# A gated linear recurrence with a dense layer behind it: the first unit's last pair of heads handled in two halves, and other rank shifts in the plan

## The chip, the cores and the metric

The kernel runs on one core of one Trainium2 chip. Such a core has five engines with a queue of instructions each: TensorE (PE, matrix products), VectorE (DVE), ScalarE (ACT), GpSimd (POOL) and SyncE (SP, which only issues transfers here). ACT and POOL issue transfers too. The metric is the device time of one execution in microseconds (us); the median of three runs is compared. The profile is of one further execution, so its own time stands beside them.

## The reference

Two layers follow each other, all in float32:

```python
# q, k, v, a_re, a_im: (4, 8, 768, 48); the state S is a complex 48x48 matrix per batch and head
mag = sqrt(a_re**2 + a_im**2);  scale = minimum(mag, 0.999) / (mag + 1e-06)
for t in range(768):
    S = (a[t] * scale[t])[:, None] * S + outer(k[t], v[t])      # a complex, k and v real
    y[t] = q[t] @ real(S)
x = y as rows of tokens                                          # (3072, 384)
out = maximum(x @ w_in, 0)**2 @ w_out                            # 384 -> 2048 -> 384
```

## The kernel before

The tokens are cut into 6 units of 512 (`L`). A unit goes through these stages:

- `load(n)`: a, q, k and v are fetched. For the first unit the weights are fetched as well, in 16 pieces of 768 KB (`fetch`, issued by POOL, line 817); they lie in memory as 64-bit floats, and `convert` turns each into float32 with one or two steps on ACT (lines 830 and 834) and two or three on DVE (lines 836, 840, 843).
- `chain(n)`: the decays are normalised (lines 936 to 982; ACT and DVE take turns, and each step waits for the one before it), multiplied together within groups of four steps (lines 992 to 1000), scanned over the whole unit (`scan`, lines 1138 to 1205, with transposes on PE, line 1046, and copies of them on ACT, lines 1061 and 1227), and applied to q and k (lines 1266 to 1280). Everything is done for two halves of the heads, z = 0 and 1.
- `pairs(n)`: the 8 heads are handled as 4 pairs. Per pair: operands are turned to the right layout (for the first two units by PE, line 1382, with copies on ACT, line 1386), score products (PE, line 1400) are masked by DVE into `A` (line 1403), `keep` makes the states `St` that are carried between the four steps of 128 tokens (PE line 1428, DVE lines 1437 and 1439; its operand `KC` is gathered by small transfers, line 1321), and `mix` forms the pair's output in one PSUM bank, `yp`: 14 products, step by step over j = 0 to 3 (lines 1452 and 1456). ACT copies `yp` to a buffer `yt` in token order (line 1462, one copy of 112 x 512), and SP sends the rows of each head to their place in `xT` (line 1470). `xT` holds the unit's activations, features on partitions, in three chunks of 128 features; the last pair of a unit ends the third chunk.
- `dense(n, grp)`: for two groups of 256 tokens, the products with w_in (PE, line 1492), relu and square on ACT (lines 1523 and 1524), and the products with w_out. In the first group of each unit some of these products run on their first two chunks before the third chunk of `xT` is there (`split`, in the first two units more of them, on spare banks). From unit 1 on, the products with w_out take halves (line 1600); in eight of the groups (`seven`) one of eight block products is saved by sums and differences that DVE forms (line 1615, results added at line 1624).

None of this stands in the order of the program. Every piece of work is a `step` of a `Plan` with an engine, an assumed duration, keys that it reads and writes, and a rank. `Plan.order` plays the steps through as a list scheduler: on the engine that can start first it takes the ready step of the lowest rank, and the instructions are then issued in that order, so that each engine's queue has a fixed order. Where PE would stop for longer than 0.8 us of the assumed time, idle matmuls on a spare bank are put in (line 735). `plan.shift` (line 1740) adds numbers to the ranks of groups of steps or of single steps, and so moves them in the queues. The real waits are set by the data, not by the plan's assumed times.

The lines of the last stage of a pair:

```python
y = take("yt", 2)
step("ACT", ac(L) + 0.5, [("yp",)], [("yt", y)], lambda: act.copy(...))      # line 1462
...
dma(sp, [("yt", y)], [("xT", n % 2, r // C)], lambda ...: sp.dma_start(...)) # line 1470
```

Of the kernel before, what the change touches and what calls it, by code (L numbers as in the profile page):

```python
# [480 lines left out]
class Plan:  # L481
# [49 lines left out]
    def order(self):  # L531
        steps = self.steps
        users = [[] for _ in steps]
        left = []
        for n, s in enumerate(steps):
            left.append(len(s[2]))
            for d in s[2]:
                users[d].append(n)
        engines = {s[0] for s in steps}
        free = {e: 0.0 for e in engines}  # L540
        wait = {e: [] for e in engines}
        done, start, at = {}, {}, {}
        bus, warm = 0.0, 6.0
        self.fill = {}

        def ready(n):
            e = steps[n][0]
            t = 0.0
            for d in steps[n][2]:
                same = steps[d][0] == e and steps[d][5] is None  # L550
                hop = 0.0 if same else self.HOP[steps[d][0]]
                if e == "PE" and not same and done[d] > 100.0:
                    paired = steps[d][5] is not None and steps[n][6]
                    hop += self.SLACK if paired else self.MARGIN
                t = max(t, done[d] + hop)
            at[n] = t
            wait[e].append(n)

        for n in range(len(steps)):
            if not left[n]:  # L560
                ready(n)
        for _ in steps:
            best = None
            for e in engines:
                if not wait[e]:
                    continue
                t = max(free[e], min(at[n] for n in wait[e]))
                if best is None or t < best[0]:
                    best = (t, e)
            t, e = best  # L570
            n = min((n for n in wait[e] if at[n] <= t), key=lambda n: (steps[n][4], n))
            wait[e].remove(n)
            _, dur, _, _, _, wire, _ = steps[n]
            start[n] = t
            if e == "PE":

                stop = t - free[e]
                spare = [b for b in self.lives if self.spare(b, done, free[e])]
                if spare and stop > self.FILL:
                    self.fill[n] = int((stop - 0.3) / self.EACH), spare[0]  # L580
                elif stop > self.STOP:
                    warm = t + self.COLD
                if t < warm:
                    dur += min(dur, 0.5 * (warm - t))
            free[e] = t + dur
            if wire is None:
                done[n] = t + dur
            else:
                lat, size = wire
                bus = max(bus, t + dur) + size / self.RATE  # L590
                done[n] = max(bus, t + dur) + lat
            for m in users[n]:
                left[m] -= 1
                if not left[m]:
                    ready(m)
        self.start, self.done = start, done
        return sorted(start, key=lambda n: (start[n], n))
# [24 lines left out]
def fast_path(ctx, tc, q, k, v, a_re, a_im, moe_w_in, moe_w_out, out, flag):  # L622
# [5 lines left out]
    B, H, S, D = q.shape  # L628
    C = 128
    W = 4  # L630
    L = W * C
    NU = B * S // L
    NP = H // 2
# [3 lines left out]
    NM = DM // C  # L637
# [12 lines left out]
    dve, pool, act, sp = nc.vector, nc.gpsimd, nc.scalar, nc.sync  # L650
    pe = nc.tensor
# [5 lines left out]
    def sb(name, n, dtype=F32, rows=C):  # L657
        return const.tile([rows, n], dtype, name=name)

    w1 = sb("w1", NM * FF).rearrange("p (i m f) -> p i m f", m=NM, f=2 * C)  # L660
# [9 lines left out]
    QT = [sb(f"QT{s}", 16 * C) for s in range(2)] + [TT[:, 0:16 * C]]  # L670
# [10 lines left out]
    St = [sb(f"St{s}", 3 * 2 * D) for s in range(2)]  # L681
    yts = [sb(f"yt{s}", L) for s in range(2)]
# [3 lines left out]
    xT = sb("xT", 2 * NM * L).rearrange("p (n m t) -> p n m t", n=2, m=NM)  # L686
# [11 lines left out]
                                                           r=2, b=2)  # L698
# [8 lines left out]
            for n in ("d0", "d1", "d2", "sc0", "sc1", "tr0", "tr1", "yp")}  # L707
    ypair = bank["yp"]
# [7 lines left out]
                     in_=turn_.rearrange("p (k x w) -> p k x w", w=4, x=4))  # L716
# [22 lines left out]
    def vs(n):  # L739
        return n % 2 if n < ROOM else 0  # L740
# [7 lines left out]
    def ac(n):  # L748
        return n / 1200.0 + 0.18
# [3 lines left out]
    def step(*args, **kw):  # L753
        return plan.add(*args, **kw)
# [4 lines left out]
    def dma(q, reads, writes, fn, rank, size, lat=1.8, group=None):  # L759
        name, dur = ("POOL", 0.55) if q is pool else ("SP" if q is sp else "ACT", 0.6)  # L760
        step(name, dur, reads, writes, fn, rank, (lat, size), group)
# [575 lines left out]
    def pairs(n, which):  # L1337
# [106 lines left out]
        def mix(i):  # L1444
            T = QT[got["T", i]].rearrange("p (i k h t) -> p i k h t", i=W, k=2, h=2)[0:R]
            at, s = got["S", i]
            aa = [As[got["A", i, h]].rearrange("p (j t) -> p j t", j=W) for h in range(2)]

            def go():
                for j in range(W):  # L1450
                    for h in range(2):
                        pe.matmul(ypair[64 * h:64 * h + D, ts(j, C)], lhsT=v5[:, j, 2 * i + h],  # L1452
                                  rhs=aa[h][:, j], start=True, stop=at[j] is None)
                    for h in range(2):
                        if at[j] is not None:
                            pe.matmul(ypair[64 * h:64 * h + D, ts(j, C)], lhsT=at[j][:, h],  # L1456
                                      rhs=T[:, j, 0, h], start=False, stop=True)
            step("PE", 2.0, [("A", got["A", i, h]) for h in range(2)]
                 + [("v", vs(n)), ("QT", got["T", i]), ("St", s), ("S", n % 2, i)],
                 [("yp",)], go, rank)  # L1460
            y = take("yt", 2)
            step("ACT", ac(L) + 0.5, [("yp",)], [("yt", y)], lambda: act.copy(  # L1462
                out=yts[y][0:64 + D].rearrange("p (j t c) -> p j c t", j=W, c=W),
                in_=ypair[0:64 + D].rearrange("p (j c t) -> p j c t", j=W, c=W)), rank)
            for h in range(2):
                r, end = (2 * i + h) * D, (2 * i + h + 1) * D
                p = 64 * h
                while r < end:
                    m = min(end - r, C - r % C)
                    dma(sp, [("yt", y)], [("xT", n % 2, r // C)], lambda r=r, m=m, p=p: sp.dma_start(  # L1470
                        out=xT[r % C:r % C + m, n % 2, r // C],
                        in_=yts[y][p:p + m]), rank, m * 2048, 2.4, group=n)
                    r, p = r + m, p + m

        for i in which:
            (turn_pe if n < EARLY else turn)(i)
# [7 lines left out]
    def dense(n, grp):  # L1484
# [14 lines left out]
        for f2 in range(NF // 2):  # L1499
# [4 lines left out]
            tiles.append((s, o.rearrange("p (f t) -> p f t", f=2)))  # L1504
            blocks.append((f2, b, ps, o, s))
        split = 3 + len(spare) if grp == 0 else 0
        for f2, b, ps, o, s in blocks[:split]:
            f = fs[f2][0]
            step("PE", 0.87, [("w1", f // FP)] + [("xT", n % 2, m) for m in range(NM - 1)],
                 [(b,)], part_of(f, ps[:, 0], range(NM - 1)), rank)  # L1510
        for f2, b, ps, o, s in blocks:
            for j in range(2):
                f = fs[f2][j]
                late = f2 < split and j == 0
                step("PE", 0.43 if late else 1.3,
                     [("w1", f // FP)] + [("xT", n % 2, m) for m in range(NM)]
                     + ([(b,)] if late or j else [])
                     + ([(b, "y")] if f2 < split and j else []),
                     [(b, "y")] if late else [(b,)] if j == 0 else [(b, "x")],
                     part_of(f, ps[:, j], (NM - 1,) if late else range(NM)), rank)  # L1520

            def relu(o=o, ps=bank[b]):
                act.activation(out=o, in_=ps, func=AF.Relu)  # L1523
                act.activation(out=o, in_=o, func=AF.Square)  # L1524
            step("ACT", 2 * ac(2 * G), [(b, "x"), (b,), (b, "y")],
                 [(b,)] + [("g", s, r) for r in range(4)], relu, (0, n))
# [209 lines left out]
    for i in range(2 * NPIECE):  # L1736
# [1 line left out]
    verdict()  # L1738

    plan.shift(  # L1740
        groups={51: 101.97, 77: 100.01, 80: 2.93, 100: -0.9, 159: -2.64, 161: 0.18, 183: 98.76,
            190: -200.92, 192: 0.69, 217: 103.2, 232: 0.28, 234: 103.28, 258: 1.25, 297: 0.64,
            352: 0.34, 354: 0.6, 372: 0.17, 394: -2.31, 396: -101.12, 411: -201.73},
        single={48: 0.43, 244: 2.93, 358: 0.46, 425: 4.98, 481: -297.85, 584: 0.23, 603: -197.29,
            731: 103.3, 809: 200.47, 856: 8.98, 911: 0.46, 1263: -97.94, 1415: -0.29,
            1677: -97.83, 1749: 1.33, 1753: 98.01, 2212: -0.63})
    with tc.manual_schedule():
        bad = plan.emit(flag[0:1, 0:1])
    return bad
# [53 lines left out]
```

## Time and profile before

| what | us |
|---|---|
| median of 3 runs | 702.49 |
| lowest and highest run | 701.89 and 705.13 |
| the profiled execution | 705.98 |
| its span, first to last instruction | 704.2 |
| PE busy | 685.2 (97%) |
| DVE busy | 572.1 (81%) |
| ACT busy | 347.9 (49%) |
| first dense product / last product | 98.99 / 697.9 |
| idle matmuls of line 735, all before 97.3 | 61.1 |

A row of a timeline gives the start and the length of a run of like instructions, the engine, the line, the operation, what it writes and reads, the count, and in brackets how long the engine sat idle before it and what ended that. Rows of PE overlap a little, since the end of a product in the pipeline is modelled. The list of waits sums such idle times by the line that waited and the work that released it: total, number of times, longest.

### The profile page before, as it was taken

The page shows a single profiled execution, that of the slowest core. Times are in us where ns is not written, and L with a number is a line of the kernel's source. Part 1 is how long each engine was busy: PE and PEld are TensorE (multiplying, and loading weights), DVE is VectorE, ACT ScalarE, POOL GpSimd, SP SyncE. Part 2 cuts the span into 40 slices and gives each one's busy share as a digit, 9 for nine tenths or more (in the row PEclk, how much of TensorE's full clock was granted, in tenths as well). Part 3 has the DMA queues.
Part 4 walks back from the last instruction along what each step waited for, and adds up shares of the span by engine and source line. Part 5 has one row for each costly group of instructions (what it writes and reads, how often), then busy time and mean ns, then how long its engine had stood idle before and what let it go on. Part 6 is the DMA issues. An engine that isn't in the chain of part 4 may idle for free.

```text
span 704.2 us, 12518 instructions
## 1 busy us (share of the span) xinstructions
PE 685.2 (97%) x4562; PEld 622.7 (88%) x4562; DVE 572.1 (81%) x1173; ACT 347.9 (49%) x578; POOL 175.7 (25%) x334
## 2 busy tenths in 40 slices
PE   9998889999999999999999999999999999999996
PEld 9998878767788999998998998998989989999996
DVE  5989899999888789997898598998599998337721
ACT  6693468955485534376424557324657242132230
POOL 6502553052400003305044050033130033032200
PEclk9999899999999999999999999999999999999999
DMA  9741459220630004735037570036550035288600
GB/s 276 220 178 26 105 133 292 76 68 20 171 104 23 1 13 123 197 78 155 0 96 197 127 154 12 1 91 179 136 158 1 19 86 136 65 282 282 208 2 27
DMA packets 56647, 79.58 MB, mean 113 GB/s; under 512 B 10976, under 2 KB 38752, under 8 KB 56576
## 3 DMA queue, kind: packets, MB, share of 16 engines
q0 software_dynamic: 15232, 40.72, 19.1%
q1 hardware_dynamic: 37072, 32.89, 18.4%
q10 hardware_dynamic: 4272, 5.08, 2.7%
q8 instruction: 38, 0.62, 0.4%
q14 instruction: 33, 0.27, 0.1%
HBM read 48.76 MB, written 4.72 MB: 76 GB/s over the span
## 4 chain that ended last, share of the span: by engine, by line
PE 63%; DVE 24%; DMA 4%; issue 3%; ACT 3%; SPq 1%; POOL 1%; ACTq 0%; DVEq 0%
PE d L1492 24%; PE d L1600 20%; PE sc L1400 4%; DVE f L1266 3%; PE d L1538 3%; DVE f L1280 3%; PE yp L1452 3%; PE tr L1428 2%; PE yp L1456 2%; DVE aq L1270 2%; PE tr L1492 1%; DMA aq<-in_a_im_dram 1%; DMA KC<-f 1%; PE sc L1492 1%; DVE f L992 1%
## 5 line engine op out<-in xcount | busy, mean ns | idle before, releaser
L1492 PE MATMUL d<-xT,w 128*128 128x256 f32 x1056 | 236.3, 381 | 3.1 <-issue 2.1
L1492 PEld LDWEIGHTS d<-xT,w 128*128 128x128 f32 x1056 | 199.0, 190 | 31.7 <-issue 3.5
L1600 PE MATMUL d<-w,g 128*128 128x192 f32 x768 | 132.7, 328 | 0.0
L1600 PEld LDWEIGHTS d<-w,g 128*128 128x128 f32 x768 | 124.9, 190 | 1.5 <-issue 0.9
L1523 ACT ACTIVATE g<-d 128x512 f32<-128x512 f32 x88 | 52.1, 592 | 120.6 <-PE d L1492 88.9
L1321 POOL DMA_DIRECT2D KC<-f x160 | 78.4, 498 | 112.0 <-issue 56.0
L1561 POOL DMA_DIRECT2D out_dram<-ot x22 | 12.6, 572 | 241.4 <-DVE ot L1624 145.1
L1600 PE MATMUL d<-T,g 128*128 128x192 f32 x384 | 66.8, 327 | 0.7 <-DVE g L1615 0.7
L1600 PEld LDWEIGHTS d<-T,g 128*128 128x128 f32 x384 | 62.8, 190 | 1.3 <-DVE g L1615 1.0
L735 PE MATMUL d<-ident 128*128 128x128 f32 x520 | 61.1, 281 | 1.5 <-POOL ident masks.py:199 1.5
L910 POOL DMA_DIRECT2D v<-in_v_dram x80 | 46.4, 587 | 64.7 <-PE yp L1452 21.0
L1524 ACT ACTIVATE g<-g 128x512 f32<-128x512 f32 x96 | 60.5, 631 | 3.0
L735 PEld LDWEIGHTS d<-ident 128*128 128x128 f32 x520 | 60.5, 198 | 1.5 <-POOL ident masks.py:199 1.5
L1615 DVE TENSOR_TENSOR g<-g 128x512 f32<-128x512 f32 x64 | 43.1, 684 | 22.3 <-ACT g L1524 15.3
L1400 PE MATMUL sc<-QT 96*128 96x128 f32 x368 | 47.9, 285 | 1.2 <-ACT QT L1386 1.2
L1462 ACT COPY yt<-yp 112x512 f32<-112x512 f32 x24 | 26.1, 1089 | 43.5 <-PE yp L1456 43.5
L1400 PEld LDWEIGHTS sc<-QT 96*128 96x128 f32 x368 | 45.0, 198 | 3.0 <-ACT QT L1386 1.6
L1266 DVE TENSOR_TENSOR f<-aq,xn 128x384 f32<-128x384 f32 (+1 forms) x64 | 45.0, 748 | 2.0 <-ACT xn L1227 1.9
L1280 DVE TENSOR_TENSOR f<-aq 128x384 f32<-128x384 f32 (+1 forms) x64 | 44.9, 752 | 0.6
L1538 PE MATMUL d<-w,g 128*128 128x384 f32 x128 | 44.3, 488 | 0.0
L1403 DVE TENSOR_TENSOR A<-sc,mask 128x512 f32<-128x512 f32 x45 | 29.7, 680 | 15.1 <-PE sc L1400 15.0
L992 DVE TENSOR_TENSOR f<-aq 128x384 f32<-128x384 f32 x72 | 36.9, 553 | 0.9
(195 smaller groups left out, 993.5 us busy)
## 6 DMA issues: line engine op xcount, KB each, us to landing
QT<-aq SPq DMA_DIRECT2D x128, 64.0 KB, 2.1
f<-in_moe_w_in_dram POOLq DMA_DIRECT2D x8, 768.0 KB, 7.1
f<-in_moe_w_out_dram POOLq DMA_DIRECT2D x8, 768.0 KB, 6.4
KC<-f POOLq DMA_DIRECT2D x104, 48.0 KB, 2.7
out_dram<-ot POOLq DMA_DIRECT2D x22, 192.0 KB, 2.4
QT<-aq ACTq DMA_DIRECT2D x64, 64.0 KB, 2.5
v<-in_v_dram POOLq DMA_DIRECT2D x80, 48.0 KB, 2.9
xT<-yt SPq DMA_DIRECT2D x36, 96.0 KB, 2.4
```

The lines of the kernel that those rows point to most:

```text
L735: plan = Plan(lambda b: pe.matmul(bank[b][:, 0:C], lhsT=ident, rhs=ident, start=True, stop=True), ["d2", "d1", "d0"], lambda ap: tc.nc.val ...
L910: lambda i=i, c=c, src=src: pool.dma_start(out=t[32 * c:32 * c + 32, i], in_=src[c]), vrank, 32 * 1536, 4.0,
L992: dve.tensor_tensor(out=f, in0=a[:, :, :, c - 1], in1=a[:, j, :, c].unsqueeze(1).to_broadcast([C, 2, HH, D]), op=ALU.mult)
L1266: lambda j=j, r=r: dve.tensor_tensor(out=f4[:, j, r], in0=a[:, r], in1=over(j), op=ALU.mult), late[z])
L1280: lambda j=j, r=r, o=o: dve.tensor_tensor(out=o[:, :, :, r * D:(r + 1) * D], in0=qk[:, j], in1=a[:, r], op=ALU.mult), late[z])
L1321: lambda i=i, c=c, queue=queue: queue.dma_start(out=kc[32 * c:32 * c + 32, i], in_=nat[32 * i:32 * i + 32, c]),
L1400: pe.matmul(sa[:, j], lhsT=T[:, j, 1, h], rhs=T[:, j, 0, h], start=True, stop=True)
L1492: pe.matmul(ps, lhsT=w1[:, f // FP, m, ts(f % FP, C)], rhs=xT[:, n % 2, m, ts(grp, G)], start=(m == 0), stop=(m == NM - 1))
L1523: act.activation(out=o, in_=ps, func=AF.Relu)
L1524: act.activation(out=o, in_=o, func=AF.Square)
L1538: pe.matmul(ps, lhsT=gt[:, f % 2, ts(i, C)], rhs=w2[:, f], start=(f == 0), stop=(f == NF - 1))
L1600: pe.matmul(bank[b][:, 0:DH], lhsT=g4[:, r, j], rhs=w(j), start=first and j == 0, stop=last and j == NT - 1)
```

## The change

- `mix`: for the first unit's last pair (`n == 0 and i == NP - 1`), the work is cut in two halves of the steps, j = 0, 1 and j = 2, 3. Each half has its own PE step, its own copy out of `yp` (112 x 256) and its own two transfers to `xT`, of 256 columns each. The rows of the second head of that pair go out on ACT's queue, not on SP's. All other pairs stay as they were.
- For the plan, `xT` gets one more key, "lower", for the third chunk's first half in the first unit; the first group of the dense layer of that unit depends on it and no longer on the whole chunk.
- The engines are gone through in a fixed order in `Plan.order`, where before it was a set.
- The numbers of `plan.shift` are others, and more: 38 groups and 28 single steps, before 20 and 17.

```diff
-        engines = {s[0] for s in steps}
+        engines = ("PE", "DVE", "POOL", "SP", "ACT")
...
+            cut = 2 if n == 0 and i == NP - 1 else 1
             y = take("yt", 2)
+            for u in range(cut):
+                js = range(u * W // cut, (u + 1) * W // cut)
+
+                def go(js=js):
+                    for j in js:
...
+                banks = [("yp", b) for b in range(2) if cut == 1 or b == u]
+                step("PE", 2.0 / cut, [("A", got["A", i, h]) for h in range(2)]
+                     + [("v", vs(n)), ("QT", got["T", i]), ("St", s), ("S", n % 2, i)],
+                     banks, go, rank)
+                sl = slice(js[0], js[-1] + 1)
+                mine = [("yt", y)] + ([("yt", y, 1)] if u else [])
+                step("ACT", ac(L // cut) + 0.5 / cut, banks + mine[:u], mine[u:], lambda sl=sl: act.copy(
+                         out=yts[y][0:64 + D].rearrange("p (j t c) -> p j c t", j=W, c=W)[:, sl],
+                         in_=ypair[0:64 + D].rearrange("p (j c t) -> p j c t", j=W, c=W)[:, sl]),
+                     rank)
+                xs = slice(js[0] * C, (js[-1] + 1) * C)
...
+                        queue = act if cut > 1 and h else sp
+                        writes = [("xT", n % 2, r // C)] if cut == 1 or u else []
+                        if n % 2 == 0 and r // C == NM - 1 and (cut == 1 or u == 0):
+                            writes.append(("xT", 0, NM - 1, "lower"))
+                        dma(queue, mine, writes,
+                            lambda r=r, m=m, p=p, xs=xs, queue=queue: queue.dma_start(
+                                out=xT[r % C:r % C + m, n % 2, r // C, xs],
+                                in_=yts[y][p:p + m, xs]), rank, m * 2048 // cut, 2.4, group=n)
...
+        def xk(m):
+            return ("xT", n % 2, m, "lower") if (n, grp, m) == (0, 0, NM - 1) else ("xT", n % 2, m)
...
-            step("PE", 0.87, [("w1", f // FP)] + [("xT", n % 2, m) for m in range(NM - 1)],
+            step("PE", 0.87, [("w1", f // FP)] + [xk(m) for m in range(NM - 1)],
...
-                     [("w1", f // FP)] + [("xT", n % 2, m) for m in range(NM)]
+                     [("w1", f // FP)] + [xk(m) for m in range(NM)]
...
     plan.shift(
-        groups={51: 101.97, 77: 100.01, 80: 2.93, 100: -0.9, 159: -2.64, 161: 0.18, 183: 98.76,
...
+        groups={9: -102.88, 43: 0.17, 51: 104.25, 54: -106, 77: 100.01, 101: -0.9, 105: 5.24,
...
```

The later lines move down with it: line 1462 becomes 1471, 1470 becomes 1486, 1492 becomes 1508, 1600 becomes 1619, 1615 becomes 1634.

## The prediction

> **What bounds the kernel now.** I read the busy shares by stage first, then the waits of TensorE, then the timelines round the first unit's last pair. The stages:
>
> ```profile
> 0.00:56.00 56.00, 54.16 (x465) 54.00 (x466) 45.28 (x105) 41.83 (x63) 22.05 (x49) 1.00 0.67 212
> 56.00:98.00 42.00, 38.15 (x360) 35.56 (x360) 38.75 (x81) 16.63 (x27) 15.68 (x32) 0.92 0.35 83
> 98.00:106.00 8.00, 5.43 (x36) 4.17 (x33) 7.86 (x11) 5.53 (x8) 7.64 (x14) 1.00 0.67 152
> 106.00:240.00 134.00, 132.07 (x727) 104.72 (x727) 118.71 (x248) 94.12 (x158) 29.38 (x53) 1.00 0.36 99
> 240.00:430.00 190.00, 188.82 (x1290) 175.93 (x1289) 166.22 (x337) 92.90 (x158) 50.59 (x96) 1.00 0.43 107
> 430.00:600.00 170.00, 168.68 (x1110) 156.72 (x1109) 149.32 (x312) 74.51 (x130) 36.20 (x70) 1.00 0.32 85
> 600.00:698.00 98.00, 97.89 (x588) 91.56 (x586) 45.65 (x87) 22.44 (x36) 14.16 (x21) 1.00 0.47 153
> ```
>
> The columns are the stretch, its length, then busy us of PE, PEld, DVE, ACT and POOL, the granted clock, the DMA share and GB/s. To 56 us PE's time is idle matmuls (line 735) and DVE works off the first unit's chain. From 106 to 698 PE is busy for 132.07 + 188.82 + 168.68 + 97.89 = 587.5 of 592 us: 4.5 us of waiting in all. DVE beside it has about 12% free until 600, so in that stretch either engine can make the other wait. A gain can come from two places only: an earlier start of the dense work near 105 us, and those 4.5 us. The start:
>
> ```profile
> 98.91 0.84 ACT L963 ACTIVATE f<-f 128x768 f32<-128x768 f32 x1 [4.37 <-DVE f L958]
> 99.66 0.83 ACT L970 ACTIVATE f<-f 128x768 f32<-128x768 f32 x1
> 100.39 1.12 ACT L1462 COPY yt<-yp 112x512 f32<-112x512 f32 x1
> ...
> 101.54 1.17 SPq L1470 DMA_DIRECT2D xT<-yt  x2
> ...
> 102.43 1.03 PE L1492 MATMUL sc<-xT,w 128*128 128x256 f32 x4
> 105.52 2.40 PE L1492 MATMUL d<-xT,w 128*128 128x256 f32 x10 [2.07 <-issue]
> ```
>
> The last mix ends at 99.07, but ACT has two steps of the next unit ahead of the copy, one of which waits for DVE (line 958). The copy ends at 101.5, the second DMA goes out at 102.1 and lands some 3.3 us later, and PE, which has done what needs only the first two chunks of xT, waits 2.07 us.
>
> **The change, part by part.** Places of after come from the order of its built instructions, durations from the trace of before.
>
> DVE up to the last pair. Before, DVE waits here:
>
> ```profile
> 36.43 0.35 DVE L1020 TENSOR_TENSOR f<-f 128x192 f32<-128x192 f32 x1 [1.17 <-issue]
> ...
> 87.47 0.25 DVE L1437 COPY St<-tr 96x96 f32<-96x96 f32 x1 [0.78 <-PE tr L1428]
> ```
>
> After puts a weight step (line 840, 0.95) into the first, and line 947 (0.94) of the next unit ahead of the second. The scan in between is longer: lines 1020 and 1026 (2.9 us together) now stand inside it, and a line 836 (0.55) ahead of the second inner chain. That 0.55 is covered, as PE's first block of idle matmuls ends only at 35.4, later than the chain at 32.9. The second block has 71 idle matmuls, not 59: 12 x 2 x 0.113 = 2.7 us more, ending at about 52.1 where the transposed operand is there at about 51.6; this 0.5 us on PE is covered by three weight steps on DVE (2.3 us). So line 1266 starts at 56.3 instead of 55.74, with one weight step more done. From there both run the same apply steps, so the last line 1280 of the unit ends at 86.65 + 0.5 = 87.15. Then after has 947 (0.88), three St steps (0.9), 843 (0.9), two mask multiplies (line 1403, 1.3): 91.1. Then one St step (0.25), 836 (0.47), 956, 958, 840 and 843 (0.9 each), and the last two mask multiplies (1.25): 96.65, against 97.27 before. By then after has line 958 (0.95) done as well, which before came after it. Total: DVE is about 1.5 us ahead.
>
> ACT. After, line 963 can start when 958 ends, 91.1 + 0.25 + 0.47 + 1.8 = 93.6, then itself (0.84), the third pair's copy (1.05), 970, 972 and 980 (0.83, 0.85, 1.07): ACT is free at 98.2. Mix begins with the masks, and a line 836 (0.5) now stands ahead of the St copies that its second step needs, so it lasts 2.2 us, not 1.9, and ends at 98.8.
>
> The halves. [...] The row: before, the 112x512 copy follows the last matmul of yp. [...] yp is one bank. As built, the first half's copy indeed waits for the last matmul of the mix and the second half's for nothing. By columns alone the first copy could start when ACT is free, at 98.2; by bank at 98.85. I take 98.85: the halved mix buys nothing. The halved copy costs about 0.55 us (between 0.52, half of 1.04, and 0.65 if a fixed part stays), so the first half is in SBUF at 99.4 instead of 101.5.
>
> The DMAs. Two become four, of half the bytes; one of each pair is on ACT's queue. [...]
>
> ```profile
> xT<-yt SPq DMA_DIRECT2D x36, 96.0 KB, 2.4
> xT<-yt SPq DMA_DIRECT2D x12, 64.0 KB, 2.1
> xT<-yt SPq DMA_DIRECT2D x12, 32.0 KB, 2.6
> ```
>
> 32 KB takes no less than 96 KB, so half a row saves no latency. I take 2.4 from issue to landing, bounds 1.9 and 4.0 (the extremes of this window). The lower half is there at 99.45 + 2.4 to 3.3 = 101.9 to 102.8, against 105.4. Price of the ACT queue: two issues of 0.6 us stand ahead of line 944 (1.5 us) of the next unit, which then ends near 102.8; DVE needs it at about 104.2, so 1.4 us of cover; without it line 947 and the last weight pieces would be late by 1.2.
>
> PE. Partial blocks start when pair 2's rows have landed, about 99.0. Three take 2.6 us, to 101.6. The fourth needs weight piece 4, which DVE finishes at 96.65 + 0.5 + 0.8 + 0.95 + 1.75 + 0.5 + 0.9 + 0.9 = 102.9, because after puts lines 974 and 977 ahead of it. So PE waits 1.3 us there, a new wait in the place of the old, and goes on to full blocks at 102.9 + 0.86 = 103.8 instead of 105.52. Start: **1.7 us earlier** (bounds 0 and 2.7: DMA at 4.0 with its issue at 101, and no wait for the weights). Later pieces come at 106.0, 107.4 and 108.8, each ahead of its block. The lower key of xT changes no wait: groups of 256 columns read what they read.
>
> Fetches on POOL: one later piece comes ahead of line 910's loads, so these end near 36 instead of 33.5; first use is at 75. DMA issues elsewhere stay as many.
>
> The new ranks after 106. PE's work is the same to the instruction, so only its 4.5 us of waiting can change:
>
> ```profile
> PE tr L1046 <- DVE xn L1205: 1.3, 2, 0.9
> PE yp L1452 <- DVE A L1403: 0.9, 3, 0.5
> PE d L1600 <- DVE g L1615: 0.7, 1, 0.7
> PE tr L1382 <- DVE St L1437: 0.7, 1, 0.7
> ```
>
> With PE 1.7 and DVE 1.5 earlier I compare how far each consumer and its producer moved in their queues. Second unit's line 1205 stands 0.9 earlier, its consumer unmoved: the wait of 0.93 falls to about 0.2. In the third unit PE's consumers of lines 1205 and 1403 stand 1.3 earlier, the producers 0 and 0.3 later: about 1.4 more of waiting. In the units after it the sums of line 1615 stand 1.6 to 5 us of DVE work later, while the products on them stay where they were to 1.3 us; part is taken up by DVE's own waits there (0.5 to 1.7 each). I put 0.5 net on that, bounds -1 and +5. Sum: -1.7 - 0.7 + 1.4 + 0.5 = -0.5, and since a wait once taken delays PE against DVE and shortens the next, the +1.4 and +0.5 count about two thirds: **-1.1 us**. The tail after 698 keeps its order. The profiled execution, 705.98 us with a span of 704.2, would become 704.9 with 703.1; the median 702.49 becomes 701.4.
>
> **Rivals.** (1) The ranks also clear the later waits: the start's 1.7 us plus 2 to 4 of the 4.5 us give 696.8 to 698.8, say 698. For it: unit 2's scan and several products move the right way. Against: DVE is as full as before. (2) Slower: the sums of line 1615. In three sevens between 400 and 520 us they were done only 0.2 to 1.8 us ahead of the product that reads them; they move back by 1.6 to 5 us of DVE work. At 2 us unhidden in each, 6 - 1.7 = 4.3 us are lost: 706.8. It decides from about 1.7 us per product group. (3) The change does nothing: DMA landing in 4.0 us or the weight piece later than 104.5 leaves the start at 105.5, with the later waits about as they were: 702.5.
>
> **How the numbers follow.** The start's gain in part (701.4): 0.38. Rival 1 (698): 0.36. Rival 2 (706.8): 0.20. Rival 3 (702.5): 0.06. The first, with a spread of its own of 2.3 us (698.9 to 703.7, from the bounds of the start and two thirds of those of the sums that lie on its side), and rival 3 are within 0.5% of 702.49, that is 3.5 us, about what a measurement of this kernel tells from no change; rival 1 is below, rival 2 above. So faster 0.36, same 0.44, slower 0.20. The predicted time is that of the likeliest, 701.4. The range for 8 in 10 reaches from the best price of rival 1 to that of rival 2, 696.8 to 706.8; what is left out is the upper half of rival 2 and what neither list has.
>
> **What would show it.** Right: the first half's copy (line 1471) starts near 98.9, right behind the last mix; PE's full blocks (line 1508) begin near 103.8, with a wait for DVE rather than for xT just ahead; PE's waits between there and the end sum to 4 to 6 us. Wrong: a copy that starts before the mix ends; landing times over 3.5 us for the half rows; waits of line 1619 for line 1634 above 3 us in sum (rival 2), or PE's waits below 2.5 (rival 1).

## The result, and the profile after

The changed kernel takes 706.45 us (median of 11 runs, 704.48 to 712.47) against 704.04 (11 runs, 701.89 to 705.67; 702.49 was the median of the first three): ratio **1.0068**, 95% interval 1.005 to 1.0086. It became slower by about 4.8 us, where a gain of 1.1 us, to 701.4, was forecast. The medians are only 2.4 us apart, because that of the changed kernel falls into the quicker of two groups of runs; the means, 708.45 and 703.83, are 4.6 us apart. The 706.45 lies inside the range of 696.8 to 706.8, but the sign is wrong, and the mechanism of the one rival that ends there is wrong too, as will be seen.

The runs of the changed kernel fall into two groups, and the mean granted clock of TensorE tells them apart: six runs at 704.5 to 706.5 us with a clock of 0.994 to 0.997, and five at 711.0 to 712.5 with 0.983 to 0.986. Their means are 705.74 and 711.71: the first group is 1.9 us above the kernel before, the second another 6.0. The profiled execution (711.0, span 709.3) is of the second group. That is not a disturbance from outside: the experiments remove and bring back these clock drops by the order of the kernel's own instructions (no clock under 0.992 where the first one puts that order back, down to 0.987 where the second brings it into the kernel before).

Two answers of the trace of the changed kernel, by stretches (columns as in the prediction: stretch, length, busy us of PE, PEld, DVE, ACT and POOL, granted clock, DMA share, GB/s). The stages of the forecast:

```profile
106.00:240.00 134.00, 132.56 (x735) 105.60 (x734) 119.30 (x253) 94.34 (x159) 30.78 (x55) 1.00 0.35 98
240.00:430.00 190.00, 189.36 (x1292) 176.07 (x1291) 166.05 (x340) 96.25 (x166) 50.59 (x96) 1.00 0.43 107
430.00:600.00 170.00, 167.34 (x1064) 155.02 (x1062) 144.80 (x297) 69.55 (x119) 36.09 (x70) 0.96 0.32 84
```

and the end of the last row in steps of 10 us:

```profile
570.00:580.00 10.00, 10.00 (x51) 8.97 (x50) 9.93 (x12) 3.70 (x7) 8.82 (x19) 1.00 0.68 176
580.00:590.00 10.00, 8.22 (x75) 7.65 (x75) 3.94 (x11) 1.15 (x2) 2.93 (x7) 0.81 0.40 108
590.00:600.00 10.00, 10.00 (x74) 9.36 (x70) 2.65 (x7) 1.07 (x1) 0.00 (x0) 0.51 0.40 98
```

To 580 us nothing is lost. Then PE stands still for 10 - 8.22 = 1.8 us, and the clock goes to half for (0.19 x 10 + 0.49 x 10) / 0.5 = 13.6 us (in the trace's record of the clock from 586.15 to 599.80), which costs up to 6.8 us of work. In the kernel before the same place looks so:

```profile
580.00:600.00 20.00, 20.00 (x192) 19.05 (x192) 16.93 (x32) 4.96 (x7) 5.85 (x12) 1.00 0.56 137
```

How far the work has come can be counted by the 96 squares of the dense layer on ACT (line 1543, before 1524). The 7th is 1.1 us earlier in the changed kernel (121.10 against 122.20), the 77th 2.5 us earlier (573.37 against 575.87), the 83rd 5.2 us later (633.40 against 628.16). So the whole loss of the profiled execution, 7.7 us, arises between the 77th and the 83rd square, where the last unit's pairs are worked on. TensorE's timeline there, changed kernel:

```profile
578.58 1.46 PE L1619 MATMUL d<-w,g 128*128 128x192 f32 x8
579.88 1.95 PE L1400 MATMUL sc<-QT 96*128 96x128 f32 x16
581.66 2.16 PE L1428 MATMUL tr<-v,KC 128*96 128x48 f32 x24
583.66 0.68 PE L1400 MATMUL sc<-QT 96*128 96x128 f32 x4
585.58 0.46 PE L1400 MATMUL sc<-QT 96*128 96x128 f32 x2 [1.25 <-DMA QT<-aq]
586.57 0.77 PE L1400 MATMUL sc<-QT 96*128 96x128 f32 x2 [0.53 <-issue]
587.27 0.67 PE L1458 MATMUL yp<-A,v 128*48 128x128 f32 x4
...
600.04 2.22 PE L1619 MATMUL d<-w,g 128*128 128x192 f32 x12
```

and the kernel before:

```profile
581.55 2.16 PE L1428 MATMUL tr<-v,KC 128*96 128x48 f32 x24
583.55 2.02 PE L1400 MATMUL sc<-QT 96*128 96x128 f32 x16
585.40 2.77 PE L1600 MATMUL d<-w,g 128*128 128x192 f32 x16
...
590.22 2.05 PE L1400 MATMUL sc<-QT 96*128 96x128 f32 x16
592.11 1.47 PE L1600 MATMUL d<-w,g 128*128 128x192 f32 x8
```

Before, two blocks of w_out (line 1600, 16 products) stand between the first pair's scores and the second's. In the changed kernel one of them stands ahead of the first pair's scores (578.58), the other behind all small products of both pairs (600.04): PE comes to the second pair's scores at 583.7, has done four of their products by 584.3, and stands still until more of their operand QT lands at 585.5. The last piece lands at 586.5, just ahead of the end of the second wait; the clock has fallen at 586.15, within that wait. In the kernel before QT's last piece for this pair lands at 588.0, later still, and nothing waits for it. After the wait four products of yp take 0.64 to 0.67 us, where they take 0.39 to 0.42 at full clock.

### The profile page after: what moved, and what is told of

It reads as the page before. It is cut to its first block, busy times and chain, and to the rows that moved or that the text cites. A ratio compares the mean times of both kernels' runs of the same rounds, so it can differ in the third digit from the quotient of the medians.

```text
span 709.3 us, 12588 instructions
## 1 busy us (share of the span) xinstructions
PE 692.6 (98%) x4582; PEld 629.9 (89%) x4582; DVE 572.2 (81%) x1173; ACT 348.5 (49%) x579; POOL 176.8 (25%) x334
## 4 chain that ended last, share of the span: by engine, by line
PE 62%; DVE 28%; issue 3%; DMA 2%; ACT 2%; POOL 1%; SPq 1%; DVEq 0%; ACTq 0%
PE d L1619 24%; PE d L1508 24%; PE sc L1400 5%; DVE f L1266 3%; PE yp L1458 3%; DVE f L1280 3%; PE tr L1428 3%; DVE f L992 2%; PE yp L1463 2%; DVE aq L1270 2%; DVE aq L977 1%; DVE w L843 1%; DVE f L1020 1%; POOL v L910 1%; DVE aq L998 1%
## 5 line engine op out<-in xcount | busy, mean ns | idle before, releaser
L735 PE MATMUL d<-ident 128*128 128x128 f32 x540 | 63.5, 281 | 1.5 <-POOL ident masks.py:199 1.5
L735 PEld LDWEIGHTS d<-ident 128*128 128x128 f32 x540 | 62.8, 197 | 1.5 <-POOL ident masks.py:199 1.5
L1400 PE MATMUL sc<-QT 96*128 96x128 f32 x368 | 49.7, 290 | 2.6 <-DMA QT<-aq 1.2
L1471 ACT COPY yt<-yp 112x512 f32<-112x512 f32 (+1 forms) x25 | 26.5, 1059 | 49.9 <-PE yp L1463 31.3
```

Source lines behind the costliest of these rows:

```text
L735: plan = Plan(lambda b: pe.matmul(bank[b][:, 0:C], lhsT=ident, rhs=ident, start=True, stop=True), ["d2", "d1", "d0"], lambda ap: tc.nc.val ...
L1400: pe.matmul(sa[:, j], lhsT=T[:, j, 1, h], rhs=T[:, j, 0, h], start=True, stop=True)
```

## Experiments

In several kernels the order of all steps is written out as a list of step numbers in `Plan.emit` instead of being planned; so one stretch of the queues can be taken from one kernel and the rest from the other, and the instructions themselves stay the same. Line numbers in these kernels are shifted by the length of that list.

**Where the loss arises: the last unit's part of PE's queue put back, and brought into the kernel before.**

```diff
         order = self.order()
+        order = self.queue(order, "PE", [      # this stretch of PE's queue, in this order
+            2063, 2283, 2307, 2279, 2281, 2065, 2066, 2285, 2303, 2305, 2070, 2332, 2309,
+            2357, 2071, 2077, 2079, 2328, 2330, 2081, 2082, 2334, 2353, 2355, 2084, 2085,
+            2359, 2086, 2087])
```

> The changed kernel with one stretch of TensorE's queue put back: in the last unit's pairs the blocks of w_out stand between the score products and the mixes again, as before (29 steps of PE; all other queues and all of the front stay as changed). Theory A (the loss arises there: PE comes to the scores before their operand has landed, waits 1.8 us among small products, and the clock then falls to half for some 13 us in about half of the runs): no granted clock under 0.99 in any run, and 1 to 3 us faster than before, ratio 0.995 to 0.999, since the first 580 us were 1 to 2.5 us ahead. Rival B (the loss is spread over the other rank shifts, or lies in the halves): ratio 1.003 or more, as the changed kernel.

Measured: 1.0007 (0.9992 to 1.0022), 704.71 us, largest of 14 runs 705.97, no clock under 0.992. Twenty-nine steps of one queue carry 0.6% of the 0.7%. The expected gain over the kernel before did not come; that is the front (below). The same stretch of the profile:

```profile
580.00:600.00 20.00, 19.74 (x189) 18.58 (x188) 10.82 (x25) 4.91 (x8) 5.45 (x12) 1.00 0.58 150
```

The other direction: the kernel before, with its own order up to the step ahead of that stretch (2234 steps), and the changed kernel's order of all queues for the 278 steps behind it.

```diff
-        order = self.order()
+        order = [...]    # before's first 2234 steps, then the rest in the changed kernel's order
```

> The kernel before, but from the last unit's first group of w_out on (around 575 us) every queue goes on in the changed kernel's order. Theory A: slower by 2 to 8 us, ratio 1.003 to 1.011, with a clock of 0.983 to 0.987 in some runs. Rival B: ratio 0.998 to 1.002 and the clock as before.

Measured: 1.0082 (1.0055 to 1.011), 709.88 us, 6 runs with clocks of 0.987 to 0.994 (0.983 to 0.987 was expected in some). The loss is in these steps and needs nothing of the front. In its profile the wait is another one:

```profile
582.94 2.16 PE L1586 MATMUL tr<-v,KC 128*96 128x48 f32 x24
588.72 2.07 PE L1558 MATMUL sc<-QT 96*128 96x128 f32 x8 [3.62 <-DVE A L1561]
```

Here the scores wait 3.6 us for DVE's masked copy of the pair before (which frees their bank), not for QT. So it is not one slow transfer: PE is at these scores before anything behind them can be ready, because the blocks that should fill the time stand later in its queue. The clock over 580 to 600 us is 0.83 here, which is 0.17 x 20 / 0.5 = 6.8 us at half: more of the loss is waiting here, and less is clock. Theory A stands as to the place, but not in that the operand QT must be the late one.

**Halves alone, ranks alone.** All queues as before, with the last pair in halves:

```diff
-        order = self.order()
+        order = [...]    # the kernel before; at its mix, copy and transfers the two halves
```

> Only the halves: the first unit's last pair is mixed, copied and moved by halves and the second head's rows go out on ScalarE's queue, while every other step keeps its place in the queues of the kernel before. Both theories: the copy of the first half still begins behind the whole mix, so the first half is in SBUF 0.5 us earlier and the second 0.1 to 0.6 later; a DMA per half and head saves 0.6 of issue. Full blocks 0.5 to 1.5 us earlier than 105.5, ratio 0.998 to 1.000. If the loss lay in the halves (part of B): ratio over 1.003.

Measured: 0.9995 (0.998 to 1.0009), 703.57. The halves are worth nothing that shows in the median. In the profile the early start is there: the first full block starts 5.3 us after the first dense product, before 6.5. (This execution was already 1.7 us ahead at that product, 97.26 against 98.99, as its half clock near 78 us lasted 3.4 us and not 6.8: a mean of 0.96 over 56 to 98 us, before 0.92.) The gain turns into another wait one block group later, on a weight piece that DVE (line 843 of the change) has not finished:

```profile
102.57 2.43 PE L1667 MATMUL d<-xT,w 128*128 128x256 f32 x10 [0.31 <-DMA xT<-yt]
106.61 1.13 PE L1667 MATMUL tr<-xT,w 128*128 128x256 f32 x4 [1.61 <-DVE w L1002]
```

And the changed kernel's order with the last pair whole:

```diff
-        order = self.order()
+        order = [...]    # the changed kernel's, without the second half's four steps
```

> Only the places in the queues: the order of all steps is that of the changed kernel, but the last pair's mix, copy and transfers are whole, on SyncE's queue. Theory A: 1.003 to 1.011, with the lower clock in part of the runs, as the changed kernel. If the loss lies in the halves: ratio 1.000 or less.

Measured: 1.0059 (1.0038 to 1.008), 707.46, up to 712.53, with clocks down to 0.983. The loss comes with the ranks.

**Is it the standing still that costs, or also what follows?** In the changed kernel the late wait is filled with 8 idle products ahead of the second pair's scores; it is not made shorter.

```diff
         order = self.order()
+        self.fill[2303] = 8, "d1"
```

> The changed kernel with 8 idle products (1.8 us) in TensorE's queue just ahead of the last unit's score products that wait for their operand. The wait is filled, not shortened. If the standing still is what lowers the clock: the half clock near 585 to 600 us is gone and with it 2 to 7 us, ratio 1.001 to 1.004. If it is the thin work (small products one after the other, with no block of w_out between): the half clock stays in part of the runs, ratio 1.006 to 1.009.

Measured: 1.0022 (1.001 to 1.0033), 705.46, largest of 21 runs 707.71, lowest clock 0.990. From 1.0068 to 1.0022 is 0.46%, 3.2 us on the mean: that is about the price of the clock alone, since the idle products shorten no wait. The mean of these runs, 705.69, is that of the changed kernel's quicker group, 705.74: the slower group is gone, and what is left, 1.8 us over the mean of the kernel before, is about the length of the wait. Profile of that kernel:

```profile
584.15 2.16 PE L1429 MATMUL tr<-v,KC 128*96 128x48 f32 x24
586.15 2.02 PE L736 MATMUL d<-ident 128*128 128x128 f32 x16
588.00 1.06 PE L1401 MATMUL sc<-QT 96*128 96x128 f32 x8
588.99 0.42 PE L1459 MATMUL yp<-A,v 128*48 128x128 f32 x4
```

and by stretches

```profile
580.00:590.00 10.00, 10.00 (x96) 9.75 (x96) 6.43 (x14) 2.44 (x5) 5.43 (x12) 1.00 0.56 157
590.00:600.00 10.00, 10.00 (x107) 9.58 (x104) 4.29 (x10) 2.49 (x3) 0.00 (x0) 1.00 0.56 132
```

From 588.0 to 595.9 only small products follow each other here too, and the clock stays at 1.00. So in this profile thin work alone did not lower it. Whether the gap itself brings the drop, or also how little PE does around it, this run does not separate; the last section sets waits and clocks side by side.

**The stretch between 125 and 575 us**, on which the forecast had put a loss:

```diff
-        order = self.order()
+        order = [...]    # before: first 526 steps and last 264; between them the changed kernel's order
```

> The kernel before with the changed kernel's order of all queues only between the first transposes of the second unit's scan (about 125 us) and the last unit's pairs (about 575 us). My forecast had 1.2 us more of waiting there: ratio 1.002. The two traces have 1.4 us less there: ratio 0.998.

Measured: 0.9985 (0.9976 to 0.9994), 702.68. The middle gains 1.1 us. The waits of PE between 106 and 580 us in the changed kernel:

```profile
PE d L1619 <- DVE ot L1643: 0.9, 1, 0.9
PE tr L1382 <- DVE St L1437: 0.8, 1, 0.8
PE tr L1046 <- ACT xn L1007: 0.5, 1, 0.5
PE yp L1458 <- DVE A L1403: 0.3, 2, 0.2
PE d L1508 <- DVE ot L1643: 0.3, 1, 0.3
```

2.8 us, against 4.3 before in the same stretch. The wait of the product for line 1634's sums is gone, and no other such wait has come.

**The front: the third pair's rows.** Two loads of the imaginary parts of a (line 896) stand ahead of the third pair's rows on SyncE's queue in the changed kernel, where one stood before; two of the real parts are ahead of them in both. The changed kernel:

```profile
96.33 5.66 SPq L1486 DMA_DIRECT2D xT<-yt  x5
99.41 0.70 PE L1508 MATMUL d<-xT,w 128*128 128x256 f32 x2
99.52 0.63 ACT L1471 COPY yt<-yp 112x256 f32<-112x256 f32 x1 [1.59 <-PE yp L1463]
100.83 0.62 ACT L1471 COPY yt<-yp 112x256 f32<-112x256 f32 x1 [0.68 <-ACT yt L1471]
101.63 2.40 PE L1508 MATMUL d<-xT,w 128*128 128x256 f32 x10 [1.53 <-DMA xT<-yt]
103.86 1.03 PE L1508 MATMUL sc<-xT,w 128*128 128x256 f32 x4
104.73 3.62 PE L1508 MATMUL d<-xT,w 128*128 128x256 f32 x16
```

The rows were copied at 95.6, but issued at 96.3 to 97.6, and the last landed at 101.7. With the mix earlier (kernel of the first experiment) the same wait is longer and the clock is at half for about 6.7 us around its end (a mean of 0.76 over 98 to 112, 0.24 x 14 / 0.5); ten products take 4.61 us, not 2.40:

```profile
97.39 0.70 PE L1532 MATMUL d<-xT,w 128*128 128x256 f32 x2
102.02 4.61 PE L1532 MATMUL d<-xT,w 128*128 128x256 f32 x10 [3.93 <-DMA xT<-yt]
```

The test: those seven transfers in another order, namely two loads, the third pair's rows, two loads (changed kernel: four loads, then the rows).

```diff
         order = self.order()
+        order = self.queue(order, "SP", [503, 504, 340, 341, 342, 505, 506])
```

> The changed kernel with two loads of the next units (line 896, the imaginary parts of a) put behind the third pair's three row transfers in SyncE's queue, so that one stretch of seven transfers is in another order. Theory F (the front gained less than forecast because PE's first blocks wait for the third pair's rows, whose transfers now stand behind two more loads, 1.5 to 3.9 us of waiting, and a wait that long lets the clock fall to half for 3.4 or 6.8 us): that wait falls under 1 us, no half clock between 96 and 112 us, 0.5 to 2 us faster than the changed kernel; the late loss stays, so ratio 1.003 to 1.006 to the kernel before. Rival (landing is slow whatever stands ahead): wait and ratio as the changed kernel, 1.0068.

Measured: 1.0038 (1.0017 to 1.0058), 706.46: the wait is 1.04 us in its profile, the clock stays at 1.00 from 98 to 112 us, and 8 of 22 runs are still at a clock of 0.988 or less, up to 712.33, as the late place is untouched. Both places put right, that is this edit and the one of the first experiment together:

> The changed kernel with both: the seven transfers of SyncE in that other order, and the last unit's stretch of TensorE's queue as in the kernel before. If the two places hold the whole loss, what is left is the gain of the other ranks and of the halves: ratio 0.995 to 0.998, that is 700.5 to 702.7, and no half clock after the first unit. If one of the two does nothing: 0.999 to 1.002.

Measured: 0.9987 (0.9974 to 1.0001), 702.72, no run over 704.83. Against the first experiment, which differs by the seven transfers alone, it is 0.2% less; there, as between the last run and the changed kernel, the intervals overlap. The forecast of 0.995 to 0.998 was missed, and the profile says where to:

```profile
98.17 3.02 PE L1534 MATMUL d<-xT,w 128*128 128x256 f32 x12
102.05 1.13 PE L1534 MATMUL sc<-xT,w 128*128 128x256 f32 x4 [0.86 <-DVE w L869]
103.98 3.69 PE L1534 MATMUL d<-xT,w 128*128 128x256 f32 x16 [0.80 <-DMA xT<-yt]
```

The first blocks no longer wait, but the fourth does for its weight piece and the full ones for the halves' rows: the first half's were issued at 98.9 and 99.2, with two loads issued just ahead of them from 97.1 on, and PE was released by them at 104.0, 4.8 us after the later issue. In the changed kernel the same half rows took 2.4 and 2.7 from issue to landing. That the loads slow whichever rows come behind them is not shown: no run moves loads alone. Over the profiles the first blocks wait 1.5 to 3.9 us with four loads ahead of the rows (four kernels), 0.3 to 1.8 with three, as before (six kernels), and none and 1.0 with two (two kernels). The fourth load costs something; the scatter is as large as the rest.

**The second queue.** What helped, together: an order written out with the front and the end of the kernel before, the halves in it as in the run with the halves alone, and the changed kernel's middle (e9; the next kernel, with one queue, is e10).

> What helped, put together: the halves of the first unit's last pair with all queues of the front and of the end as in the kernel before, and the changed kernel's order between about 125 and 575 us. The parts alone measured 0.9995 (halves) and 0.9985 (middle). If they add: 0.997 to 0.999, about 702.4, with no half clock near 590 us. If the halves only move a wait: 0.9985 as the middle alone.

Measured: 1.0002 (0.999 to 1.0014), 703.95: by the points the halves take back what the middle gives; the interval just overlaps that of the middle alone. The same with the second head's rows on SyncE's queue:

```diff
-                        queue = act if cut > 1 and h else sp
+                        queue = sp
```

> As e9, but the second head's half rows go out on SyncE's queue behind the first head's, as in the kernel before. By the rows of the trace an issue takes 0.6 us: the later half's second transfer goes out 0.6 us later, and ScalarE is free for the next unit 1.2 us sooner. Within 0.1% of e9 if the queue is worth only its issue.

Measured: 0.9985 (0.9974 to 0.9996), 702.80. The point is 0.17% lower, more than the 0.1% expected; the intervals overlap a little. The two profiles show a mechanism. With two queues ACT issues a transfer after each copy, and gets to the next unit's first step (line 944 of the change) late; the weight piece (843) that DVE ends behind it is late for PE:

```profile
102.56 1.47 ACT L1102 ACTIVATE f<-aq 128x1536 f32<-128x1536 f32 x1
106.40 1.13 PE L1666 MATMUL tr<-xT,w 128*128 128x256 f32 x4 [2.05 <-DVE w L1001]
```

with one queue

```profile
100.78 1.47 ACT L1102 ACTIVATE f<-aq 128x1536 f32<-128x1536 f32 x1
105.76 1.13 PE L1666 MATMUL tr<-xT,w 128*128 128x256 f32 x4 [1.52 <-DVE w L1001]
```

ACT is 1.8 us later, DVE's weight pieces behind it 0.6. In the version with both places put right the same edit was tried:

> The version with the two stretches of queue put right (the third pair's rows ahead of two loads on SyncE's queue, the w_out blocks between the last unit's small products), and in addition all four half-row transfers on SyncE's queue. That version measured 0.9987; taking the second head's rows off ScalarE's queue was worth 0.17% where the front was that of the kernel before (1.0002 against 0.9985). If that holds here too: 0.997, about 702. If it was chance, or belongs to that front alone: 0.998 to 1.000.

Measured: 0.9995 (0.9985 to 1.0005), 702.76. No gain there, so the price of the second queue belongs to the one front, or is smaller than these intervals.

**Idle products in the front's waits of e9 (e11):**

```diff
-        self.fill = {110: (142, 'd2'), 142: (59, 'd2'), 145: (4, 'd2'), 218: (53, 'd2'), 359: (2, 'd2')}
+        self.fill = {110: (142, 'd2'), 142: (59, 'd2'), 145: (4, 'd2'), 218: (53, 'd2'), 359: (2, 'd2'),
+                     404: (4, 'd1'), 411: (8, 'yp')}
```

> As e9, with idle products in TensorE's queue at the two places where it stands still for xT after the last mix: 4 (0.9 us) ahead of the first block of the dense layer and 8 (1.8 us) ahead of the first full block. If standing still there lowers the clock in part of the runs, as the half clock at 100 to 109 us in several profiles says, these are gone: no run over 704.5 and 0.5 to 1 us less than e9. If not: the same as e9, or up to 0.5 us more where the rows are there before the idle products end.

Measured: 0.999 (0.9977 to 1.0002), 703.60, largest 705.64. Inconclusive: 0.12% under its partner, inside both intervals, and the largest run is not lower.

No kernel beats the kernel before by more than about 0.15%. The two that are below it beyond their intervals are the middle alone (702.68) and the middle with halves on one queue (702.80).

## Why the prediction was wrong, step by step

- **What bounds the kernel.** Right that TensorE is the bound from 106 us on and that only its waits can change. Wrong in what was left out: the sum took the clock as 1.00 after 98 us because the rows of before showed it so. The same table showed 0.92 between 56 and 98 us: the clock was at half from 77.5 to 84.3, behind waits of PE of 0.94 and 0.47 us, on KC, that end at 75.1 and 76.1, and within one of 0.37 us, on ACT. What a new wait does to the clock was put at nothing. That is the largest missing term: 3.2 us on the mean (filled wait against open wait).
- **The new ranks after 106.** I compared PE's consumers with DVE's producers only, from the second unit on, and put +1.2 us net on it, +0.6 after the discount to two thirds. Measured there: -1.1 us (the middle alone), waits 2.8 instead of 4.3. The wait of line 1205 went as forecast (0.9 to none), the +1.4 of the third unit and the +0.5 of the sums did not come.
- **The last unit's pairs.** Not looked at. PE's own order there moved (the blocks of w_out from between the small products to both sides of them), with QT's transfers and DVE's masks about as they were. It costs 0.6% by the run that puts it back and 0.8% by the run that brings it into the kernel before. This is the step that failed: "so only its 4.5 us of waiting can change" was followed by a list of PE's waits for DVE, and neither a wait that did not exist before nor a transfer was in it. In its place came a new wait of 1.8 us, on QT, with half clock behind it. The sign "PE's waits between there and the end sum to 4 to 6 us" was met, with 2.8 + 1.8 = 4.6, but by luck: 1.8 us of it lie where none was forecast.
- **The start.** Forecast 1.7 us earlier; the profiled execution shows 0.8 (full blocks at 104.73 against 105.52). The copies came as said: the first behind the last product of the mix (99.52, the mix ending at 99.48), 0.63 us each (0.52 to 0.65 said), half rows landed 2.4 and 2.7 us after issue (2.4 taken), at 102.5 and 102.9 (101.9 to 102.8 said). What failed is "partial blocks start when pair 2's rows have landed, about 99.0": they landed at 100.1 to 101.7, with one more load ahead of them. That wait, 1.5 to 3.9 us in the profiles of that front, took the place of the one removed; the wait for the weight piece, which I had put there, is hidden behind it and appears (0.86) when it is cleared. In other executions the clock falls in this gap too (0.76 over 98 to 112 us in the kernel of the first experiment), and then the front gains nothing: full blocks at 107.52 there. The front of the kernel before is not free of this: in the profiles of two kernels that have it (the end of the changed kernel, and its middle, brought into the kernel before) waits of 3.5 and 4.0 us in sum there come with about 3.4 us of half clock (0.88 over 98 to 112 us in both).
- **The halved mix** buys nothing by itself: right, by the copy's start and by the run with the halves alone (0.9995). The wait of the first copy for the whole mix is in the kernel as built; whether a copy could run beside the mix was not tried.
- **The ACT queue.** The forecast's cover of 1.4 us was roughly enough for line 947 in the changed kernel. In the front of the kernel before it was not: 1.8 us on ACT, 0.6 on the weight piece. That a second issuing engine would save the time of issuing (0.53 to 0.61 us a transfer on ACT's queue) and no more was an estimate; no run shows a saving from the second queue (1.0002 with it and 0.9985 without in one front, 0.9987 and 0.9995, within the intervals, in the other).
- **Rival 2 (706.8)** has nearly the measured time and a false mechanism: the products wait 0.0 us for line 1634, before 0.7.

The sum by runs: end +0.61% (the changed kernel against the run that puts the stretch back), middle -0.15%, and the front with the halves +0.22% as what is left (1.0007 less 0.9985). The last has an interval of about 0.2% and its parts are not settled; what it is made of stays open.

## What to carry to other kernels

Where one engine is busy to 99%, look at its own queue for places where small dependent products follow each other without long independent blocks between them, and check each operand there, transfers included, against the time at which the queue will arrive. A wait on TensorE can have two prices, its length (here about 1.8 us) and what the clock does behind it (here 6.0 us more in five of eleven runs); idle products in the wait paid the first and avoided the second (lowest clock 0.990 in 21 runs). Moving the rows up in SyncE's queue moved the wait to other rows and to a weight piece, so count the queue as a whole.

## What the runs showed of the chip

In the profile of the changed kernel two waits of 1.25 and 0.53 us, 1.8 in sum within 2.3 us and among small products, came with half clock for 13.65 us (586.15 to 599.80) that began within the second. Near 78 us half clock lasted 6.8 us in both kernels, behind or within waits of 0.94, 0.47 and 0.37 us in the kernel before and of 0.49 and 0.30 us in the changed one.

The waits in the front and the clock beside them, one profile each (waits of PE between the first block and the full blocks; mean granted clock over 98 to 112 us; half clock worked out from it, (1 - clock) x 14 / 0.5):

| kernel | waits, us | clock | half clock, us |
|---|---|---|---|
| before | 0.50, 2.07 | 1.00 | none |
| changed | 1.53 | 1.00 | none |
| PE's late queue put back | 3.93 | 0.76 | 6.7 |
| before, with the end of the changed kernel | 0.30, 3.21 | 0.88 | 3.4 |
| ranks alone | 2.69 | 0.88 | 3.4 |
| rows ahead of loads | 1.04, 0.86 | 1.00 | none |
| idle products in the late wait | 2.31 | 0.88 | 3.4 |
| before, with the middle of the changed kernel | 1.75, 2.25 | 0.88 | 3.4 |

The length of a wait alone does not decide: one of 2.07 us left the clock at 1.00, those of 1.25 and 0.53 us at the late place did not. Here the changed kernel at that place, 3.41 us ahead of the drop and 3.41 behind it:

```profile
582.74:586.15 3.41, 2.06 (x19) 1.70 (x18) 2.31 (x8) 0.00 (x0) 0.19 (x1) 1.00 0.39 94
586.15:589.56 3.41, 2.99 (x24) 2.77 (x26) 0.00 (x0) 0.00 (x0) 0.00 (x0) 0.50 0.00 0
```

and the kernel before at its wait of 2.07 us in the front, which ends at 105.5:

```profile
101.40:104.81 3.41, 2.05 (x10) 1.47 (x8) 3.34 (x5) 3.04 (x6) 3.41 (x7) 1.00 0.66 145
104.81:108.23 3.42, 2.71 (x12) 2.19 (x13) 3.42 (x4) 1.25 (x2) 3.42 (x7) 1.00 1.08 209
```

PE was busy for 2.06 us of 3.41 in the one and for 2.05 in the other, the first with small products, the second with blocks of 128x256; only behind the first did the clock fall. Nor does the program decide: the mean clock of the changed kernel is 0.983 to 0.986 in five runs and 0.994 to 0.997 in six. What does decide is not shown by these runs, and neither is the part that the kind of products plays.
